# Two stores of a weight pipeline moved: sums stored a step after their last split, down weights handled two steps later

## The chip, the core and the metric

The kernel runs on one core of a Trainium2 chip. A core has a matrix engine (TensorE, PE in the profile), a vector engine (DVE), a scalar engine (ACT), GpSimd (POOL) and SyncE (SP), which here issues nearly all DMA transfers. Every engine works through its own list of instructions in order and waits at semaphores for the others; the transfers themselves run on 16 DMA engines beside them. The metric is the time of one execution on the device, in microseconds (us); lower is better.

## What is computed

Two layers of the same kind on an activation x of 2048 rows by 640 columns. Each layer is a Fourier mixing block followed by a gated feed-forward block, both with a residual:

```python
def _A_ref(x, dft_seq_re, dft_seq_im, dft_hid_re, dft_hid_im):
    a = jnp.einsum("bsd,ed->bse", x, dft_hid_re)
    b = jnp.einsum("bsd,ed->bse", x, dft_hid_im)
    return jnp.einsum("ts,bse->bte", dft_seq_re, a) - jnp.einsum("ts,bse->bte", dft_seq_im, b)

def _B_ref(x, w_gate, w_up, w_down):
    g = jnp.einsum("bsd,df->bsf", x, w_gate)
    u = jnp.einsum("bsd,df->bsf", x, w_up)
    return jnp.einsum("bsf,fd->bsd", _sigmoid(g) * u, w_down)

for layer in range(2):
    x = x + _A_ref(_layernorm(x), dft_seq_re, dft_seq_im, dft_hid_re, dft_hid_im)
    x = x + _B_ref(_layernorm(x), w_gate, w_up, w_down)
```

The hidden size of the feed-forward block is F = 1728: 13 tiles of 128 columns (j = 0 to 12) and a tail of 64 (j = 13). The weights are the same in both layers.

## The kernel before

**Precision by parts.** All large products run in f16 with each f32 number split in a high part HI and a rest LO; a product is three matmuls, HI by HI, HI by LO and LO by HI. `split` (L231 to 238) makes the parts of a weight: HI by one ACT instruction (L236), LO by one DVE instruction (L238).

**Blocks.** The feed-forward block treats the 2048 rows in four blocks of 512. In the first block of a layer, block 0, `gate_up` (matmuls at L1049) multiplies the rows with the gate and up weights themselves, one hidden tile j to a step: 30 matmuls of 512 columns for j below 13 and 15 for the tail; the first two of a step use the gate weight's HI part and the third is the first that needs its LO part. ACT then takes the sigmoid (L1063), DVE the product with the up half (L1064), and `gated_parts` splits the result into f16 (L1073 on ACT, L1074 on DVE) as tile `ht` of the hidden activation. Then `down` (L1242) multiplies the 14 hidden tiles with the down weights in eight steps, two for each 128 rows, and adds to x (L1257). In blocks 1 to 3, `seven` (L1095) forms gate and up with fewer products, from combinations of the weights, the "sums".

**What block 0 of the first layer does on the side.** It prepares every weight for the whole kernel:
- `load_w` fetches the f32 gate and up tiles (L954), the tail (L952) and the down tiles (L956, L959); `split_w` splits them; `keep_w` (and `gate_up` itself for gate and up) stores the f16 parts to DRAM as `kept_w`, through `keep` (L254).
- `make_sums` forms four sums of 256 columns of each gate and up tile on POOL (L998 to L1001), `split_sums` splits them in two pieces of 256 and 768 columns (L236, L238 again), and `keep` stores them as `kept_s`. For j of 3 to 12 the sums and their f16 parts have two fixed buffers each, by j even or odd (`take_sums`); the f32 gate and up tile is given back when its sums are made.

The same engines finish the mixing block beside it: `combine` (L920), `join_hidden` (L927) and `add_hidden` (L940) on DVE add its last rows to x, with a copy of one row on POOL (L938) between L940's first and second part. The tail of the hidden tiles is gated in `gate_tail` (L1225 to L1229).

Later blocks and the second layer only fetch `kept_w` and `kept_s` again (`load_s`, L1020 to L1023, and `load_w_again`). Before block 1 its activations are normalized, split and turned by DMA transposes (L516).

**What sets the order.** There is no automatic scheduler. `at(u, f, ...)` puts a job at a due time u, counted in steps; a loop at the end goes through the steps and, ahead of each step's matmuls, emits the jobs due in it, sorted by u. A gate/up step of block 0 has number `block[0] + j`. In the first layer the steps of j = 0 to 2 are written out by hand in an opening, so j = 3 is step 0, and jobs due earlier fall into step 0 as well. On each engine instructions stand in the order of emission, and so do the transfers in SP's queue: one that waits for its data keeps all that are behind it.

**Slots.** Most buffers come from one pool, `Slots`: `take` gives the free place that has been free longest among a few candidates, `drop` gives it back. A buffer's first writer so waits for whoever read the place last, which may be a store. Which places are used depends on the order of the jobs.

Due times before, with j the tile: gate/up loads at `block[0] + j - 4` and splits at `block[0] + j - 2` (j from 5 on); sums made at u = `block[0] + j - 1.5`, split at u + 1.55 (ACT) and u + 1.9 (DVE), stored in the same job; down loads at `block[0] + 0.8 j - 0.5`, splits at `+ 0.8 j + 1.6`, stores at `+ j + 4`.

All tiles on the chip are views of one large buffer, so the profile calls nearly all of them `big`.

Of the kernel before, what the change touches and what calls it, by code (L numbers as in the profile page):

```python
# [178 lines left out]
@with_exitstack  # L179
def kernel(ctx: ExitStack, tc: tile.TileContext, x, ct, wh, wg, wu, wc, wd, out):  # L180
    nc = tc.nc
    pool = ctx.enter_context(tc.tile_pool(name="sb", bufs=1))
    psum = ctx.enter_context(tc.tile_pool(name="ps", bufs=1, space=bass.MemoryType.PSUM))
    dram = ctx.enter_context(tc.tile_pool(name="dr", bufs=1, space=bass.MemoryType.DRAM))

    big = pool.tile([P, (UNITS + 2 * CK) * UNIT], F32, name="big")
    acc = [psum.tile([P, 512], F32, name=f"acc{i}") for i in range(6)]
    flag = pool.tile([P, 1], I32, name="flag")
    with tc.manual_schedule():
        folded(ctx, tc, pool, dram, big, acc, flag, x, ct, wh, wg, wu, wc, wd, out)  # L190
    bad = nc.values_load(flag[0:1, 0:1], min_val=0, max_val=1,
                         skip_runtime_bounds_check_because="it is the result of a comparison")
    with tc.If(bad != 0):
        with tc.manual_schedule():
            general(tc, big, [acc[2 * i : 2 * i + 2] for i in range(4)], x, ct, wh, wg, wu, wc, wd, out)


def folded(ctx, tc, pool, dram, big, acc, flag, x, ct, wh, wg, wu, wc, wd, out):
# [34 lines left out]
    def split(dh, dl, src, s, do=ALL):  # L233

        if 0 in do:
            nc.scalar.activation(dh, src, AF.Copy, scale=s)  # L236
        if 1 in do:
            nc.vector.scalar_tensor_tensor(dl, src, s, dh, op0=OP.mult, op1=OP.subtract)  # L238
# [13 lines left out]
    def keep(v, *key):  # L252
        kept[key] = dram.tile(list(v.shape), F16, name="kept_" + "_".join(map(str, key)))
        nc.sync.dma_start(kept[key], v)  # L254
# [5 lines left out]
    def at(u, f, *a):  # L260
        jobs[max(0, int(u // 1))].append((u, f, a))

    held = {}
# [16 lines left out]
    def drop(*key):  # L280
        s = held.pop(key if len(key) > 1 else key[0])
        if s.span:
            slots.give(s)
# [703 lines left out]
    def take_sums(key, j):  # L987

        if 3 <= j < NF:
            return fixed(XU + XTU + 16 * (j % 2) + 8 * (key == "sp"), 8, key, j)  # L990
        return take(8, key, j)
# [13 lines left out]
    def split_sums(j, do):  # L1005
        v, w = held["sf", j].f32, take_sums("sp", j) if 0 in do else held["sp", j]
        h, l = w.parts
        for c, sign in ((slice(0, 256), -WS), (slice(256, 1024), WS)):
            split(h[:, c], l[:, c], v[:, c], sign, do)
        if 1 not in do:  # L1010
            return
        drop("sf", j)
        keep(w.f16, "s", j)
        if j < 3:
            held["S", j] = held.pop(("sp", j))
        else:
            drop("sp", j)

    def load_s(j):
        nc.sync.dma_start(take(5, "G", j).f16, kept["w", 0, j])  # L1020
# [446 lines left out]
    for layer in range(2):  # L1467
# [10 lines left out]
        block = []  # L1478
# [81 lines left out]
        for b in range(1, NB):  # L1560
            for i in range(2):
                u = block[b] - 8 + 1.2 * i
# [9 lines left out]
        for b in range(NB):  # L1572
            for j in range(NF + 1):
                for q in ((0, j), (1, j)) if j < NF else ((3, 0),):
                    u = block[b] + j
# [12 lines left out]
            at(block[0] + j + (1.6 if j > 2 else 1.3), gated_parts, j)  # L1588
        for j in range(NF + 1):
            if first:  # L1590
                at(block[0] + 0.8 * j - 0.5, load_w, 2, j)
                at(block[0] + 0.8 * j + 1.6, split_w, 2, j)
                at(block[0] + j + 4, keep_w, 2, j)
            else:
                at(block[0] + j, load_w_again, 2, j)
                at(block[1] + j - 0.3, test_w, 2, j)

        if first:
            for j in range(NF):
                if 3 <= j < NF:  # L1600
                    u = block[0] + j - 1.5
                else:
                    u = block[1] - 8 + 1.5 * j
                    at(u - 2, load_sums, j)
                at(u, make_sums, j)
                at(u + 1.55, split_sums, j, (0,))
                at(u + 1.9, split_sums, j, (1,))
            at(block[0] + 12, close_slots)


# [8 lines left out]
        for q, (load, test, key) in enumerate(tests):  # L1619
            u = u0 + pace * q  # L1620
# [186 lines left out]
```

## Time and profile before

| | |
|---|---|
| median of three runs | 1168.69 us (1167.34 to 1170.28) |
| the profiled execution | 1166.17 us, span of the instructions 1164.4 us |
| mean granted TensorE clock in it | 0.995 |
| PE busy | 1128.2 us, 97% of the span |
| DVE, ACT, POOL busy | 738.8, 508.0, 149.5 us |
| moved by DMA | 216.40 MB, mean 186 GB/s |

Block 0 of the first layer stands on the time line from about 110 us (j = 3) to 184 us (start of the down steps); block 1 begins at 228.7 us.

How to read what follows. An entry of the timeline is start, duration, engine, source line, operation, tiles and how many instructions were merged; in square brackets stands how long the engine was idle ahead of it and what released it. SPq is SyncE's queue: an entry there is the issue of a transfer, not the transfer. An entry of the waits is engine and line, what was waited for, total us, how many times, the longest. A row of the windows is the stretch, its length, busy time of PE, PEld (weight loads), DVE, ACT and POOL with the number of instructions in brackets, the granted clock of TensorE, the busy share of the DMA engines and GB/s. Line numbers are those of the kernel before; in the changed kernel lines from L1013 on shift by two, and by four near the end.

### The profile page before, as it was taken

To read this page: it belongs to the slowest core of one execution; us is meant where nothing else is said; L and a number is where in the kernel's file an instruction comes from. 1 tells how busy PE (TensorE), PEld (TensorE's weight loads), DVE (VectorE), ACT (ScalarE), POOL (GpSimd) and SP (SyncE) were. 2 spreads that over 40 slices of the span, in tenths; PEclk is the share of its full clock that TensorE was granted. 3 is DMA by queue.
4 is the path that set the end of the run, shared out by engine and by line. 5 is a ranking of instruction groups with operands and counts; after the bars stand their busy time and mean duration, and the time that the engine had idled before them with its cause. 6 is when DMAs were issued, how large, how long until landed. Compare 5 with 4: busy or idle time off the path is not lost.

```text
span 1164.4 us, 22633 instructions
## 1 busy us (share of the span) xinstructions
PE 1128.2 (97%) x8784; PEld 859.6 (74%) x8784; DVE 738.8 (63%) x1636; ACT 508.0 (44%) x1094; POOL 149.5 (13%) x269
## 2 busy tenths in 40 slices
PE   5699999999999999999999999999999999999997
PEld 2467346788878887888776844678887888788875
DVE  7996698668656776676427566746974557524530
ACT  6865474155524653365304422315552455225420
POOL 2312486110001010100000001000000001000000
PEclk9999999999999999999999999999999999999998
DMA  9417698849595977769305442787849683667301
GB/s 275 138 46 231 228 350 295 240 136 262 160 240 149 263 211 192 220 222 253 94 1 169 169 129 67 197 236 229 253 148 243 223 268 133 139 211 236 121 18 38
DMA packets 225621, 216.40 MB, mean 186 GB/s; under 512 B 68034, under 2 KB 181851, under 8 KB 225502
## 3 DMA queue, kind: packets, MB, share of 16 engines
q1 hardware_dynamic: 224862, 212.23, 61.5%
q0 software_dynamic: 640, 2.62, 0.6%
q8 instruction: 71, 1.16, 0.4%
q14 instruction: 48, 0.39, 0.1%
HBM read 171.03 MB, written 30.40 MB: 173 GB/s over the span
## 4 chain that ended last, share of the span: by engine, by line
PE 93%; DVE 3%; DMA 2%; POOL 1%; SPq 1%; ACT 0%; issue 0%; DVEq 0%; POOLq 0%
PE acc L1095 40%; PE acc L1242 31%; PE acc L1049 14%; PE acc L855 4%; PE acc L1178 2%; PE acc L773 2%; DVE big L238 1%; DMA big<-in_ct 1%; DMA big<-in_x 1%; DMA big<-in_wh 1%; PE acc L523 0%; DMA big<-in_wd 0%; POOL quad L372 0%; DVE big L627 0%; DVE big L664 0%
## 5 line engine op out<-in xcount | busy, mean ns | idle before, releaser
L1095 PE MATMUL acc<-big 128*128 128x256 f16 x4212 | 463.1, 273 | 0.1
L1095 PEld LDWEIGHTS <-big 128*128 128x128 f16 x4212 | 412.0, 98 | 48.6 <-DMA big<-kept_w 0.3
L1242 PE MATMUL acc<-big 128*128 128x320 f16 x2624 | 357.7, 299 | 0.0
L1242 PEld LDWEIGHTS <-big 128*128 128x128 f16 x2624 | 256.7, 98 | 99.7
L1099 ACT ACTIVATE big<-acc 128x256 f32<-128x256 f32 x312 | 116.6, 381 | 208.8 <-PE acc L1095 207.4
L1049 PE MATMUL acc<-big 128*128 128x512 f16 (+1 forms) x990 | 178.1, 342 | 4.6 <-DVE big L238 4.6
L1049 PEld LDWEIGHTS <-big 128*128 128x128 f16 x990 | 96.9, 98 | 84.9 <-DVE big L238 5.6
L1275 ACT ACTIVATE big<-big 128x768 f32<-128x768 f32 (+8 forms) x104 | 79.4, 764 | 124.9 <-DVE big L1300 91.2
L1163 DVE TENSOR_TENSOR big<-big 128x512 f16<-128x512 f32 x78 | 53.8, 690 | 109.2 <-ACT big L1162 109.2
L1257 DVE SCALAR_TENSOR_TENSOR big<-acc,big 128x320 f32<-128x320 f32 x64 | 28.4, 484 | 93.5 <-PE acc L1242 93.4
L238 DVE SCALAR_TENSOR_TENSOR big<-big 128x640 f16<-128x640 f32 (+6 forms) x81 | 64.9, 842 | 0.5 <-ACT big L236 0.4
L1141 ACT ACTIVATE big<-big 128x512 f32<-128x512 f32 x78 | 47.8, 627 | 37.2 <-DVE big L1132 36.9
L1297 DVE TENSOR_TENSOR big<-big 128x256 f32<-128x256 f32 x64 | 26.6, 416 | 49.8 <-DMA big<-in_ct 49.8
L1132 DVE TENSOR_TENSOR big<-big,acc 128x512 f32<-128x512 f32 x78 | 53.1, 681 | 4.2 <-PE acc L1095 4.0
L1151 DVE SCALAR_TENSOR_TENSOR big<-acc,big 128x256 f32<-128x256 f32 x78 | 32.6, 418 | 35.1 <-PE acc L1095 30.8
L236 ACT ACTIVATE big<-big 128x640 f16<-128x640 f32 (+7 forms) x81 | 49.6, 664 | 6.7 <-POOL big L998 4.3
L1162 ACT ACTIVATE big<-big 128x512 f16<-128x512 f32 x78 | 48.8, 625 | 6.5 <-DVE big L1153 5.6
L855 PE MATMUL acc<-big 128*128 128x321 f16 (+3 forms) x324 | 49.0, 300 | 1.1 <-DVE big L238 1.1
L1064 DVE SCALAR_TENSOR_TENSOR big<-acc,big 128x512 f32<-128x512 f32 x26 | 17.9, 687 | 40.4 <-PE acc L1049 28.5
L855 PEld LDWEIGHTS <-big 128*128 128x128 f16 (+3 forms) x324 | 28.2, 95 | 20.3 <-issue 7.7
L509 ACT ACTIVATE big<-big 128x384 f16<-128x384 f32 (+2 forms) x48 | 28.9, 647 | 31.0 <-DVE big L491 26.7
L1063 ACT ACTIVATE big<-acc 128x512 f32<-128x512 f32 x26 | 15.4, 592 | 57.6 <-DVE big L1074 27.2
(183 smaller groups left out, 1001.5 us busy)
## 6 DMA issues: line engine op xcount, KB each, us to landing
big<-kept_w SPq DMA_DIRECT2D x125, 320.0 KB
big<-kept_s SPq DMA_DIRECT2D x75, 512.0 KB
big<-in_ct SPq DMA_DIRECT2D x256, 128.0 KB
big<-kept_w SPq DMA_DIRECT2D x78, 192.0 KB
kept_w<-big SPq DMA_DIRECT2D x41, 320.0 KB
big<-in_ct SPq DMA_DIRECT2D x32, 256.0 KB
kept_s<-big SPq DMA_DIRECT2D x13, 512.0 KB
big<-in_wg SPq DMA_DIRECT2D x16, 320.0 KB
```

The lines of the kernel that those rows point to most:

```text
L236: nc.scalar.activation(dh, src, AF.Copy, scale=s)
L238: nc.vector.scalar_tensor_tensor(dl, src, s, dh, op0=OP.mult, op1=OP.subtract)
L855: nc.tensor.matmul(ps[:m, :EC], z[:, at : at + m], w[:, 384 * wp : 384 * wp + EC], start=(d == 0 and zp == HI and wp == HI), stop=(d == ND ...
L1049: nc.tensor.matmul(ps, w[wp][:, d * P : (d + 1) * P], xt[:, xp, :], start=(d == 0 and wp == HI and xp == HI), stop=(d == ND - 1 and wp == LO))
L1095: nc.tensor.matmul(ps, wt, xt, start=start and n == 0, stop=n == len(todo) - 1, skip_group_check=not start)
L1099: nc.scalar.activation(dst, ps, AF.Copy)
L1132: nc.vector.tensor_tensor(v, v, other, op=OP.add)
L1141: nc.scalar.activation(v, v, AF.Sigmoid, scale=SG)
L1162: nc.scalar.activation(s.parts[HI], v, AF.Copy)
L1163: nc.vector.tensor_tensor(s.parts[LO], v, s.parts[HI], op=OP.subtract)
L1242: nc.tensor.matmul(held["pd", e][0][:, :EH], held["ht", j].parts[hp][:, i * P : (i + 1) * P], held["w", 2, j].parts[wp][:, e * EH : (e + 1 ...
L1275: nc.scalar.activation(v, v, AF.Square, accum_out=new_sum()[:p])
```

## The change

Two edits, both in the first layer's block 0. The number of instructions and transfers stays the same.

1. The store of the sums of j = 3 to 12 is taken out of the job that makes their last split and becomes a job of its own, `keep_sums`, due one step later. The buffer of the split sums is released with it. For j below 3 nothing changes.
2. The down weights' loads, splits and stores get later due times: at j = 0 by 2.7, 2.6 and 1.5 steps, at j = 13 by 2.0, 1.9 and 1.5.

```diff
         drop("sf", j)
-        keep(w.f16, "s", j)
         if j < 3:
             held["S", j] = held.pop(("sp", j))
-        else:
-            drop("sp", j)
+            keep(w.f16, "s", j)
+
+    def keep_sums(j):
+        keep(held["sp", j].f16, "s", j)
+        drop("sp", j)
...
             if first:
-                at(block[0] + 0.8 * j - 0.5, load_w, 2, j)
-                at(block[0] + 0.8 * j + 1.6, split_w, 2, j)
-                at(block[0] + j + 4, keep_w, 2, j)
+                at(block[0] + 0.75 * j + 2.2, load_w, 2, j)
+                at(block[0] + 0.75 * j + 4.2, split_w, 2, j)
+                at(block[0] + j + 5.5, keep_w, 2, j)
...
                 at(u + 1.9, split_sums, j, (1,))
+                if j > 2:
+                    at(u + 2.9, keep_sums, j)
```

## The prediction

> **What bounds the kernel.** I read the page's engine shares and chain first, then PE's waits in the first layer's block 0, then back from each wait along DVE, ACT and SyncE's queue.
>
> ```profile
> PE 1128.2 (97%) x8784; PEld 859.6 (74%) x8784; DVE 738.8 (63%) x1636; ACT 508.0 (44%) x1094; POOL 149.5 (13%) x269
> PE 93%; DVE 3%; DMA 2%; POOL 1%; SPq 1%; ACT 0%; issue 0%; DVEq 0%; POOLq 0%
> PE twin L350 <- ACT big L356: 11.2, 5, 7.7
> PE acc L1049 <- DVE big L238: 4.6, 2, 2.8
> ```
>
> TensorE sets the end. Of its waits, the transposes at L350 lie in the opening, which the change leaves alone. Waits of L1049 on L238 (gate/up products waiting for a weight's LO split on DVE) are the only ones in block 0; after 184 us the list of PE's waits is empty. So the change can win no more than what is lost here, and a loss needs a new PE wait.
>
> ```profile
> 96.43 39.59 PE L1049 MATMUL acc<-big 128*128 128x256 f16 x242
> 137.87 6.65 PE L1049 MATMUL acc<-big 128*128 128x512 f16 x30 [1.84 <-DVE big L238]
> 147.31 37.04 PE L1049 MATMUL acc<-big 128*128 128x512 f16 x163 [2.80 <-DVE big L238]
> 184.19 44.72 PE L1242 MATMUL acc<-big 128*128 128x320 f16 x328
> 144.00:148.00 4.00, 1.20 (x7) 0.36 (x6) 4.00 (x8) 1.44 (x3) 0.00 (x0) 1.00 1.02 360
> 148.00:152.00 4.00, 4.00 (x12) 1.48 (x11) 4.00 (x7) 2.58 (x5) 3.59 (x2) 0.57 0.74 253
> 152.00:156.00 4.00, 4.00 (x20) 1.84 (x19) 2.60 (x5) 0.72 (x2) 3.85 (x2) 1.00 1.00 352
> ```
>
> The 163 matmuls behind the second gap are 28 of j=8, 30 each of j=9 to 12, and 15 of the tail; so the gaps stand at the first LO matmul of j=7 and of j=8. In the windows (PE, PEld, DVE, ACT, POOL busy, then clock, DMA share, GB/s) the gap has a second price: from 148 to 152 the granted clock is 0.57, with 12 matmuls where the next 4 us hold 20. That costs 4.00 x (1 - 0.57) = 1.7 us. A step of 30 matmuls takes (37.04 - 1.7) / 163 x 30 = 6.5 us.
>
> [...]
>
> **Why DVE is late.** Queue issues, then ACT, DVE and POOL:
>
> ```profile
> SPq L254 <- DVE big L238: 20.4, 4, 8.2
> SPq L956 <- DVE big L920: 9.4, 2, 8.9
> 100.92 11.57 SPq L956 DMA_DIRECT2D big<-in_wd  x5
> 119.58 0.33 SPq L254 DMA_DIRECT2D kept_s<-big  x1
> 120.43 1.31 SPq L254 DMA_DIRECT2D kept_w<-big  x2
> 121.79 0.53 SPq L954 DMA_DIRECT2D big<-in_wg  x1
> 132.84 0.33 SPq L254 DMA_DIRECT2D kept_s<-big  x1
> 113.80 0.62 ACT L1073 ACTIVATE big<-big 128x512 f16<-128x512 f32 x1
> 125.47 0.60 ACT L1063 ACTIVATE big<-acc 128x512 f32<-128x512 f32 x1 [11.06 <-DMA kept_w<-big]
> 126.10 0.69 DVE L1064 SCALAR_TENSOR_TENSOR big<-acc,big 128x512 f32<-128x512 f32 x1 [6.59 <-ACT big L1063]
> 118.23 1.29 DVE L238 SCALAR_TENSOR_TENSOR big<-big 128x256 f16<-128x256 f32 x2
> 136.40 0.68 DVE L1064 SCALAR_TENSOR_TENSOR big<-acc,big 128x512 f32<-128x512 f32 x1
> 137.00 2.75 DVE L238 SCALAR_TENSOR_TENSOR big<-big 128x640 f16<-128x640 f32 x4
> 143.69 0.89 DVE L940 TENSOR_TENSOR big<-big 128x321 f32<-128x321 f32 x2 [2.07 <-POOL big L938]
> 132.02 1.37 POOL L998 TENSOR_TENSOR big<-big 128x256 f32<-128x256 f32 x1 [2.08 <-DVE big L238]
> 135.87 1.19 POOL L1001 TENSOR_TENSOR big<-big 128x256 f32<-128x256 f32 x1
> ```
>
> Read it backwards. The splits PE wanted at 136.02 began at 137.00, behind the gate product of j=4 at 136.40. That chain had started with the sigmoid of j=3 at 125.47, though PE had done j=3 by 136.0 - 0.4 - 3 x 6.5 = 116.1: its output slot is the one that w(1,3) leaves, and the store of that weight was not out. This store stood in SP's queue behind the first store of sums, which held the queue for DVE's split at 118.23, and behind five down-weight loads, two of which waited 9.4 us for L920. SP waits in order, so one early store of sums keeps a store that was ready long before; it went out at 120.43 and landed some 5.0 us on.
>
> **The change, part by part.**
>
> *Store of sums j (j of 3 to 12) a step on.* Ten issues, none added. By the built order, kept_w(3) (two stores) and the load of j=8 now stand ahead of kept_s(3), behind only three down-weight loads, whose slots don't wait for L920. Five issues took 11.57 - 9.4 = 2.2 us, three take 1.3; so kept_w(3) goes out at about 102.3 and lands by 107.3, ahead of 116.1. The sigmoid of j=3 is then bound by PE: 125.47 - 116.1 = 9.4 us earlier; DVE, whose work is the same, by its idle of 6.59 at least. Both gaps vanish if the split of j=8 comes 1.84 + 2.80 = 4.64 us earlier against PE. I take the lead between 6.6 and 9.4, so both go.
>
> What is late next? L940 on DVE waits for the row copy L938, which stands behind the sums of j=7 on POOL. One set of sums takes 135.87 + 1.19 - 132.02 = 5.0 us. The sums of j=5 start with the split of sums 3 (about 117), the copy follows, then j=6 and j=7: 117 + 3 x 5.0 + 2 x 0.7 = 133.4, where the trace has 143.69. Behind it on DVE stand L940, L1074, one down split, L1064 and the first split of w(8), four of 0.7 to 0.8 and one 0.9: about 137.4. PE wants it at 136.02 + 6.5 + 0.4 = 142.9. The margin is 5 us.
>
> The edit also adds a wait: the buffer of sums j is free a step later, so ACT's split of sums j+2 may stand for the store of j, behind the load of j+5, which waits for POOL's sums j+2. Behind it on ACT lie the down split, L1073 and L1063. One round is 5.0 (POOL) + 1.0 (issues) + 5.0 (landing, as of kept_w) + about 2 (HI split, first LO) = 13 us, against two PE steps of 13.0: even, with the lead in hand. I cost it at nothing; the ends are 0 (the buffer is never free earlier, so no gain) and rival E. On SP itself a down store, a down load and kept_w(j+1) are queued behind the store of sums j: fewer waits than before, since its split is a step old.
>
> *Down weights: loads, splits and stores two steps on.* Fourteen each, none added; each weight's split still stands two steps behind its load, so a late load would hold ACT at L236 with the sigmoid behind it. The latest by the allocator's slots is the load of down tile 7, behind POOL's sums of j=8: the split of sums 6 follows w(8) at about 139, sums 8 end at 144, and its split stands in the step of j=9, which begins at 136.02 + 2 x 6.5 = 149. Three splits that stood in step 0 ahead of sums 3 move behind it, so sums 3 is split some 2.4 us earlier, and DVE has as much more to do in the steady steps. The cover:
>
> ```profile
> L238 DVE SCALAR_TENSOR_TENSOR big<-big 128x640 f16<-128x640 f32 (+6 forms) x81 | 64.9, 842 | 0.5 <-ACT big L236 0.4
> 110.00:194.00 84.00, 79.36 (x387) 37.94 (x386) 68.58 (x93) 49.69 (x91) 53.22 (x58) 0.98 0.77 280
> 100.00:138.00 38.00, 36.16 (x212) 20.52 (x211) 22.13 (x34) 15.95 (x28) 9.04 (x9) 1.00 0.53 189
> 138.00:176.00 38.00, 35.20 (x156) 15.41 (x155) 34.51 (x44) 27.49 (x53) 29.64 (x25) 0.96 0.96 346
> 191.72 1.20 DVE L1229 TENSOR_TENSOR big<-big 64x512 f16<-64x512 f32 x1 [0.69 <-ACT big L1227]
> 186.15 0.63 ACT L1073 ACTIVATE big<-big 128x512 f16<-128x512 f32 x1 [3.84 <-DMA kept_w<-big]
> 210.86 7.27 SPq L516 DMA_TRANSPOSE big<-big  x2
> 219.36 0.48 SPq L1020 DMA_DIRECT2D big<-kept_w  x1
> ```
>
> DVE is busy 68.6 us from 110 to 194. If PE ends the block 6.3 us earlier, the same work has 77.7: 9.1 us of idle are allowed, where I count some 5 for the copy. At the block's end PE begins j=13 of the first row tile at 184.19 + 78 x 0.136 = 194.8 (0.136 = 44.72 / 328) and DVE had the tail ready at 192.92: 1.9 us of slack. This tail must come earlier too. It can: ACT stood 3.84 us for the store of w(1,11), behind a store of sums that is now behind it. If that cover fails, three splits of 0.84, 2.5 us, are lost.
>
> The DMA engines idled half the time before 138 and were full after it (0.96). The five early loads become three, which uses the idle stretch worse (2 x 0.33 MB); the freed loads and stores use it better. At 346 GB/s a moved store is 0.33 / 346 = 0.95 us of transfer. Later stores of down weights fall among the loads for block 1, whose first is issued at 219.36, 9.3 us ahead of PE's need; one store now stands behind it that stood ahead. Taken as nothing; ends 0 and, for three stores, 2.9 us.
>
> ACT's down splits move with DVE's and have more room (49.7 us busy in the 84). POOL's queue is unchanged. Slots in later blocks have other earlier holders; the trace's nearest row for what such a slot or load can cost PE is this:
>
> ```profile
> L1095 PEld LDWEIGHTS <-big 128*128 128x128 f16 x4212 | 412.0, 98 | 48.6 <-DMA big<-kept_w 0.3
> ```
>
> 0.3 us on a load, none on PE's own row; I take 0, with 0.3 either way.
>
> **Sum.** -1.84 - 2.80 - 1.7 = -6.3 us. The profiled execution is 1166.17 (span 1164.4), 2.5 below the median 1168.69; -6.3 makes 1159.9 there and 1162.4 on the median.
>
> **Rivals.**
> A, forecast: 1162.4; own range 1160.2 to 1164.
> [...]
> C, the lead is eaten by the copy on POOL or at the seam: the 1.84 goes, a wait like 2.80 with its slow clock stays, at j=8 or at the down steps: 1166.9. For it: only 1.9 us of slack at the tail, DMA 0.96 full.
> D, SP stands as long at other items (loads waiting for POOL's sums), so that nothing reaches PE: 1168.7. Against it: kept_w(3) passes everything that held it.
> E, slower: the buffer of sums. If a store of sums lands after 9 us and not 5, a round is 17 against 13; five rounds lose 20 us, less the 11 between a weight split's turn and its use (two steps, less 1.6 for two splits): 9 us of waits, in two gaps with 1.7 of slow clock each, so 12.4 over A, 1174.8. It eats A's gain from a landing of 7.8 us (5 x 2.8 - 11 + 3.4 = 6.4). Against it: the one landing that the trace prices is 5.0.
>
> **How the numbers follow.** Chances: A 0.60, B 0.08, C 0.12, D 0.06, E 0.14. A change under 0.3% (3.5 us) can't be told from none. Faster: B and A less 0.01 for its upper end, 0.67; same: C, D and that, 0.19; slower 0.14. The range holds A, B and C with 1.5 us of spread: 1160.2 to 1168.4.
>
> **What would show it.** After: L1049's waits on L238 gone or under 1 us; clock 1.00 across block 0; the sigmoid of j=3 near 116 and its DMA wait gone; kept_w(3) issued near 102; PE reaching the down steps (184.19) near 178 and block 1 (228.74) near 222.5. Wrong, if PE waits at 135 to 180 on L238 again, at L1242 for a down split or the tail, or at L1095 for block 1's loads or transposes; if ACT's L236 stands for kept_s, it is E.

## The result and the profile after

The changed kernel takes 1164.83 us (median of 22 runs, 1160.76 to 1169.09), the kernel before on the same chips 1167.19 (22 runs, 1165.46 to 1170.28). The ratio is 0.9977 with a 95% interval of 0.9966 to 0.9987: a gain of 2.4 us, where 6.3 were forecast and 1162.4 us expected. The profiled execution took 1161.90 us, 4.3 less than the one of before.

TensorE's time line of the changed kernel, from block 0 of the first layer to the last down steps (start, duration, what, and in brackets the idle time ahead with its releaser):

```profile
96.28 78.01 PE L1051 MATMUL acc<-big 128*128 128x256 f16 x420
174.65 0.60 PE L1051 MATMUL acc<-big 128*128 128x512 f16 x2 [0.36 <-ACT big L236]
175.51 2.98 PE L1051 MATMUL acc<-big 128*128 128x512 f16 x13 [0.26 <-DVE big L238]
178.32 44.72 PE L1244 MATMUL acc<-big 128*128 128x320 f16 x328
222.88 17.30 PE L1097 MATMUL acc<-big 128*128 128x256 f16 x157
...
407.25 13.93 PE L1097 MATMUL acc<-big 128*128 128x256 f16 x126 [1.45 <-DVE small L416]
...
1106.81 44.72 PE L1244 MATMUL acc<-big 128*128 128x320 f16 x328
```

Both waits of before (1.84 at j = 7, 2.80 at j = 8) are gone: 420 matmuls, up to the end of j = 12, run without a gap. Two things are new: 0.62 us at the tail's weights (j = 13), for ACT's HI split first, and 1.45 us in block 2 (the row names DVE; the same place in other profiles names a load of weights). The window in which the granted clock was 0.57 now has 1.00 and 20 matmuls:

```profile
148.00:152.00 4.00, 4.00 (x20) 1.85 (x19) 4.00 (x5) 2.62 (x5) 3.92 (x4) 1.00 0.78 267
```

The start of that is as the prediction put it. SyncE's queue and ACT in the changed kernel:

```profile
102.15 1.39 SPq L956 DMA_DIRECT2D big<-in_wd  x3
104.00 1.10 SPq L254 DMA_DIRECT2D kept_w<-big  x2
117.21 0.33 SPq L254 DMA_DIRECT2D kept_s<-big  x1
116.05 0.60 ACT L1065 ACTIVATE big<-acc 128x512 f32<-128x512 f32 x1 [3.67 <-PE acc L1051]
```

The store of w(1,3) leaves at 104.00, ahead of the first store of sums, and the sigmoid of j = 3 starts at 116.05, released by PE and no longer by a store. The down steps begin at 178.32 (184.19 before).

So this execution gained 5.87 us in block 0 and lost 1.45 in block 2. All profiles here can be read by three places. The first is the start of the first down steps. The second is PE's waits from there to the last down steps: less these, that stretch has 927.0 to 927.4 us in every profile but one (after: 1106.81 - 178.32 - 1.45 = 927.04; before: 1111.48 - 184.19 = 927.29; in the one with 929.0, that of the last eight late below, the 126 matmuls behind a wait of 3.12 take 15.60 us and not 13.9). The third is the end, from the start of the last down steps to the end of the execution: 1161.90 - 1106.81 = 55.1 after, 1166.17 - 1111.48 = 54.7 before. The question is why the median gained so much less than this execution.

### The profile page after: what moved, and what is told of

Same layout as the page of the kernel before. It is cut to its first block, busy times and chain, and to the rows that moved or that the text cites. A ratio compares the mean times of both kernels' runs of the same rounds, so it can differ in the third digit from the quotient of the medians.

```text
span 1160.1 us, 22627 instructions
## 1 busy us (share of the span) xinstructions
PE 1127.3 (97%) x8784; PEld 859.6 (74%) x8784; DVE 737.6 (64%) x1636; ACT 508.2 (44%) x1094; POOL 147.6 (13%) x269
## 4 chain that ended last, share of the span: by engine, by line
PE 81%; DMA 3%; POOL 2%; DVE 1%; issue 1%; ACT 1%; SPq 0%; POOLq 0%; DVEq 0%; ACTq 0%
PE acc L1097 36%; PE acc L1244 31%; PE acc L1051 8%; PE acc L855 2%; PE acc L1180 2%; PE acc L773 1%; DMA big<-kept_w 1%; DMA big<-in_ct 1%; POOL big L999 1%; POOL big L1000 1%; DMA kept_s<-big 1%; DVE big L238 0%; POOL big L998 0%; POOL big L1001 0%; DMA big<-kept_s 0%
## 5 line engine op out<-in xcount | busy, mean ns | idle before, releaser
L1101 ACT ACTIVATE big<-acc 128x256 f32<-128x256 f32 x312 | 116.1, 381 | 200.1 <-PE acc L1097 198.5
L236 ACT ACTIVATE big<-big 128x640 f16<-128x640 f32 (+7 forms) x81 | 50.7, 665 | 17.0 <-DMA kept_s<-big 7.7
L773 PE MATMUL acc<-big 128*128 128x256 f16 (+5 forms) x288 | 36.9, 288 | 2.6 <-DVE big L664 2.6
```

Source lines behind the costliest of these rows:

```text
L773: nc.tensor.matmul(o, xv[:, 384 * xp + c0 : 384 * xp + c0 + n], moving(r, cps[cp]), start=(i % 2 == 0 and r == 0 and xp == HI and cp == HI ...
L1101: nc.scalar.activation(dst, ps, AF.Copy)
```

## The experiments

All ratios are against the kernel before on the same chip, with 95% intervals; its medians there were 1167.82, 1168.10 and 1167.40 us in the three groups.

### Each edit alone, and both kernels again

The first edit alone: the kernel before with `keep_sums` and its due time, the down weights at their old times.

```diff
-                at(block[0] + 0.75 * j + 2.2, load_w, 2, j)
-                at(block[0] + 0.75 * j + 4.2, split_w, 2, j)
-                at(block[0] + j + 5.5, keep_w, 2, j)
+                at(block[0] + 0.8 * j - 0.5, load_w, 2, j)
+                at(block[0] + 0.8 * j + 1.6, split_w, 2, j)
+                at(block[0] + j + 4, keep_w, 2, j)
```

> The store of sums a step later alone, down weights as before. Theory one (the store of sums was what held SyncE's queue): kept_w(3) goes out when the five down loads let it, near 113, the sigmoid of j=3 starts by 119 where it was 125.5, PE's waits in block 0 fall from 4.6 us to under 1.5 and the down steps begin by 180.5; time 3 to 5 us below before in the profile. Rival (the down loads' own wait is what counts): waits of 3 us or more stay, time within 1.5 us of before.

The second edit alone: the kernel before with the three later due times (the diff above read backwards, without `keep_sums`).

> The down weights two steps later alone, the store of sums in the same job as its split, as before. Theory one: the store of sums 3 still stands ahead of kept_w(3) and of the load of j=8 and holds them to about 117.5, the sigmoid of j=3 starts near 122, later stores of sums hold the queue as before; one wait of 1 to 3 us stays in block 0; time 0 to 3.5 us below before. Rival: the down weights carry the gain, both waits go, the down steps begin near 178.

The changed kernel again, unedited, on the same chip:

> The changed kernel once more, for a second profile. Theory one: PE reaches the down steps of block 0 near 178 again, and what is missing between the 5.9 us won there and the measured gain is lost after block 0, at waits of PE on a weight load in blocks 1 to 3, which vary from run to run (0 to 4 us). Rival: in other executions the two waits of block 0 come back and the down steps begin at 180 or later.

And the kernel before again:

> The kernel before once more, for a second profile and for what the runs of one kernel differ by. Theory one: waits of 4 to 5 us in block 0 again with a stretch of half clock behind them, down steps near 184, at most 0.5 us of waits afterwards; ratio 1.000 within 0.15%. Rival: the waits in block 0 differ by more than 1.5 us between executions.

| kernel | median us | ratio |
|---|---|---|
| first edit alone | 1159.39 | 0.9922 [0.9907, 0.9937] |
| second edit alone | 1172.87 | 1.0042 [1.0025, 1.0058] |
| both | 1162.63 | 0.9950 [0.9935, 0.9965] |
| before | 1167.12 | 0.9996 [0.9985, 1.0007] |

The edits pull in opposite directions. The first gains 8.4 us against its group's 1167.82; the second loses 5.1 alone and 3.2 on top of the first. The sign of the second edit is clear: no run of the first edit alone (up to 1160.53) reaches those of both (from 1162.10). The sizes are less so: the changed kernel's own two ratios, 0.9977 above and 0.9950 here, lie 3 us apart with intervals that don't meet. TensorE in the first edit alone, then SyncE and ACT:

```profile
96.26 81.49 PE L1051 MATMUL acc<-big 128*128 128x256 f16 x435
177.59 44.72 PE L1244 MATMUL acc<-big 128*128 128x320 f16 x328
...
407.78 13.92 PE L1097 MATMUL acc<-big 128*128 128x256 f16 x126 [2.71 <-DMA big<-kept_w]
...
1107.33 44.72 PE L1244 MATMUL acc<-big 128*128 128x320 f16 x328
```

```profile
101.37 13.58 SPq L956 DMA_DIRECT2D big<-in_wd  x6
115.00 0.90 SPq L254 DMA_DIRECT2D kept_w<-big  x2
119.68 0.60 ACT L1065 ACTIVATE big<-acc 128x512 f32<-128x512 f32 x1 [5.44 <-DMA kept_w<-big]
```

Block 0 has no wait at all, though here the store of w(1,3) still stands behind six down loads (13.58 us, most of it a wait for L920) and the sigmoid of j = 3 still waits 5.44 us for it. Passing the store of sums alone brings the sigmoid from 125.47 to 119.68, 5.8 us, and that is enough for the 4.64 that PE lacked. The down steps begin 184.19 - 177.59 = 6.6 us earlier. So theory one holds, with a gain above its 3 to 5 us: 1166.17 - 1160.53 = 5.6 in the profile, 8.4 in the median.

Another 1.5 to 1.7 us lie at the end: its profile of 1160.53 us has 1160.53 - 1107.33 = 53.2 us there, where the kernel before has 54.7 and 54.9. This goes by kernel and not by execution: 54.7 to 55.7 in eight profiles (the kernel before twice, the second edit alone, the changed kernel twice, and below the third buffer in it, the late loads and the half sums), 53.0 to 53.3 in six (the first edit alone, and below the five others built on it). It lies behind the last store, which is issued at 1152.08 of a span of 1160.1 in the changed kernel and at 1152.61 of 1158.7 in the first edit alone. The page also lists the packets of a queue of the kind "instruction" (q14). The longer end goes with 48 of them and the shorter with 46 or 47, in thirteen of the fourteen profiles (the kernel with the late stores has 48 and the short end). That it is the cause wasn't tried. If the end is no effect of the schedule, which isn't shown either, these 1.9 us are to be taken off when schedules are compared: the second edit then costs 3.2 - 1.9 = 1.3 us on top of the first here.

The second edit alone keeps the gap at j = 8 (2.80 before, 2.66 here) and adds waits at j = 12, at the tail and, last, where the down steps reach the tail of the hidden tiles:

```profile
145.01 25.64 PE L1049 MATMUL acc<-big 128*128 128x512 f16 x118 [2.66 <-DVE big L238]
171.94 0.60 PE L1049 MATMUL acc<-big 128*128 128x512 f16 x2 [1.29 <-ACT big L236]
180.70 0.60 PE L1049 MATMUL acc<-big 128*128 128x512 f16 x2 [1.68 <-ACT big L236]
198.70 34.12 PE L1242 MATMUL acc<-big 128*128 128x320 f16 x250 [1.94 <-DVE big L1229]
```

Neither expectation of it holds. One of the two gaps stays, as theory one has it, but the time is 5.1 us longer and not up to 3.5 shorter.

The kernel before, profiled again, has gaps of 1.95 us at j = 7 and 1.12 at j = 8, and two later waits of 1.73 and 1.01 us. In block 0 that is 1.6 us less than in its first profile, and it is more than 0.5 us afterwards, so here its rival comes out.

The profiled execution of the changed kernel in this group was its longest one there (1167.55 us, where the median is 1162.63), and shows what a long execution has more than the first profile:

```profile
170.70 0.60 PE L1051 MATMUL acc<-big 128*128 128x512 f16 x2 [2.79 <-ACT big L236]
171.80 8.34 PE L1051 MATMUL acc<-big 128*128 128x512 f16 x30 [0.49 <-DVE big L238]
183.13 44.72 PE L1244 MATMUL acc<-big 128*128 128x320 f16 x328
```

The two gaps of before stay away, but the down steps begin at 183.13, so what this execution lacks is lost in block 0 (the rival) and not only behind it: at j = 12 ACT's split is 2.79 us late, and the 30 matmuls behind it take 8.34 us instead of 6.5. The two executions part at the second of POOL's sums of j = 8. POOL, SyncE and ACT of this execution, and then of the first profile:

```profile
144.12 4.64 POOL L999 TENSOR_TENSOR big<-big 128x256 f32<-128x256 f32 x1
151.51 0.33 SPq L956 DMA_DIRECT2D big<-in_wd  x1
163.90 1.78 ACT L236 ACTIVATE big<-big 128x256 f16<-128x256 f32 x3 [4.24 <-DMA kept_s<-big]
```

```profile
144.01 2.10 POOL L999 TENSOR_TENSOR big<-big 128x256 f32<-128x256 f32 x1
148.28 0.33 SPq L956 DMA_DIRECT2D big<-in_wd  x1
159.09 1.77 ACT L236 ACTIVATE big<-big 128x256 f16<-128x256 f32 x3 [1.33 <-DMA kept_s<-big]
```

A down weight's load waits in SyncE's queue for these sums (6.9 us in the longer execution), the stores of sums wait behind it, and ACT's split of later sums waits for the store of earlier ones. From that wait of 4.24 us to the late split at j = 12 ACT has no idle time left. This is the wait of rival E, the buffer of sums, and in this execution it costs 2.79 + 0.49 us of gaps and 1.8 of slow matmuls. In the first profile the same wait is 1.33 us and costs nothing; what is lost there is 0.62 us at the tail, where ACT's sigmoid ahead of the split waits for POOL:

```profile
173.37 0.60 ACT L1065 ACTIVATE big<-acc 128x512 f32<-128x512 f32 x1 [2.43 <-POOL big L1000]
```

### A third buffer for the split sums

In the changed kernel and in the first edit alone, the split sums take turns over three places instead of two.

```diff
-            return fixed(XU + XTU + 16 * (j % 2) + 8 * (key == "sp"), 8, key, j)
+            if key == "sp":
+                return fixed((XU + 20, XU + XTU + 8, XU + XTU + 24)[j % 3], 8, key, j)
+            return fixed(XU + XTU + 16 * (j % 2), 8, key, j)
```

> The changed kernel with a third buffer for the split sums, so that ACT's split of sums j+2 waits for the store of sums j-1 and no longer for that of sums j. Theory S (the late sums buffer is what the changed kernel loses against the first edit alone): ACT's waits at L236 for kept_s (7.7 us in the changed kernel's profile) vanish, PE has no wait above 0.5 us in block 0, the down steps begin near 178, and the median is 1159 to 1160.5. Rival L (the down weights' later loads and splits fill ACT, DVE and SP's queue in the last steps themselves): the median stays at 1162 to 1165, and ACT or DVE is late at j of 10 to 12 for another reason than kept_s.

> The first edit alone with a third buffer for the split sums. The first edit alone has 10.6 us of ACT's waits at L236 for kept_s, and no wait of PE in block 0, so both theories expect these waits of ACT to go and the time to stay at that of the first edit alone: 1158.5 to 1160.5.

ACT's waits at L236 for `kept_s` vanished in both, yet the changed kernel with it took 1164.61 us (ratio 0.9978 [0.9964, 0.9993]; without it 0.9977 and 0.9950). TensorE and one of ACT's waits (total, times, longest):

```profile
176.59 0.60 PE L1053 MATMUL acc<-big 128*128 128x512 f16 x2 [1.69 <-ACT big L236]
177.45 4.64 PE L1053 MATMUL acc<-big 128*128 128x512 f16 x13 [0.25 <-DVE big L238]
181.92 44.72 PE L1246 MATMUL acc<-big 128*128 128x320 f16 x328
```

```profile
ACT big L1067 <- POOL big L1002: 2.4, 1, 2.4
```

Theory S falls as an account of the whole loss: the wait at the tail is there without any wait for a store of sums, and the 13 matmuls behind it take 4.64 us instead of 2.98. ACT is late because the sigmoid (L1067 in this kernel, where the line of POOL is L1002 and not L1000) ahead of the tail's split waits 2.4 us for POOL, as it did in the first profile. The first edit alone with the third buffer took 1162.38 (0.9955 [0.9940, 0.9969]), 3 more than without and above the range of both theories. Its profile, of its shortest run at 1158.25, has no wait in block 0 and a granted clock of 0.999; the other four runs had 0.995 to 0.996 and took 1162.15 to 1163.92 us; where they lost the time stays open. As the third buffer so costs something of its own, it can't price the waits for `kept_s` in the changed kernel.

### Which part of the second edit costs

On top of the first edit: the later stores alone; then the later loads and splits alone.

```diff
-                at(block[0] + j + 4, keep_w, 2, j)
+                at(block[0] + j + 5.5, keep_w, 2, j)
```

> The first edit, and of the second only the down weights' stores 1.5 steps later; their loads and splits at their old times. Theory S: the stores pass nothing that ACT waits for, except that more of them stand ahead of the late kept_s: 1159 to 1160.5, as the first edit alone. Rival L: the same, since loads and splits are what it blames. A result of 1162 or more would say that the stores cost by themselves (up to 2.9 us, three stores among the loads for block 1).

```diff
+                at(block[0] + 0.75 * j + 2.2, load_w, 2, j)
+                at(block[0] + 0.75 * j + 4.2, split_w, 2, j)
+                at(block[0] + max(j + 4, 0.75 * j + 4.5), keep_w, 2, j)
```

> The first edit, and of the second only the down weights' loads and splits; their stores at the old time. Both theories place the loss in the loads and splits: 1162 to 1165, as the changed kernel, with ACT waiting at L236 for kept_s or DVE late at j of 10 to 12. A result of 1159 to 1160.5 would say that the stores make the loss.

Stores late: 1160.43 (0.9934 [0.9919, 0.9949]), as expected and not to be told from the first edit alone. Loads and splits late: 1164.46 (0.9973 [0.9957, 0.9989]), in the range expected and 4.0 more; by the two profiles 2.1 of them lie at the end (55.35 against 53.29), which leaves 1.9 for the blocks. Then these were divided by tiles (the lines shown for tiles 0 to 5; the second kernel has `j > 5`):

```diff
+                moved = j < 6
+                at(block[0] + (0.75 * j + 2.2 if moved else 0.8 * j - 0.5), load_w, 2, j)
+                at(block[0] + (0.75 * j + 4.2 if moved else 0.8 * j + 1.6), split_w, 2, j)
+                at(block[0] + j + 5.5, keep_w, 2, j)
```

> The first edit and the later stores; of the down weights, tiles 0 to 5 are loaded and split late as in the change, tiles 6 to 13 at their old times. Theory I (what costs is that the early tiles leave the stretch from 110 to 130 us in which DVE, ACT and the DMA engines have time): 1162 to 1165, DVE busy some 7 of 10 us from 120 to 130 and a wait of PE in the last steps. Theory T (what costs is that the last tiles stand ahead of the last weight splits): 1160 to 1161, as with the later stores alone (1160.4).

> The complement: tiles 6 to 13 are loaded and split late, tiles 0 to 5 at their old times. Theory I: 1160 to 1161, no wait of PE in block 0. Theory T: 1162 to 1165, with PE waiting for the tail's split behind ACT's sigmoid that waits for POOL.

The last eight late: 1160.07 (0.9934 [0.9914, 0.9954]), nothing lost. The first six late: 1168.61 (1.0017 [1.0002, 1.0031]), 8.5 above its complement with the same short end. That is beyond theory I's 1162 to 1165 and more than the whole second edit loses; here tiles 3 to 5 also fall among tiles 6 to 8, which kept their times, so the order among the tiles seems to count too. Theory I has the place right: it is the early tiles. What they leave is seen in the windows; first the first edit alone, then the changed kernel (the last two columns are DMA share and GB/s):

```profile
110.00:130.00 20.00, 20.00 (x94) 9.09 (x93) 18.15 (x28) 9.79 (x18) 7.45 (x8) 1.00 0.61 208
130.00:160.00 30.00, 29.94 (x140) 13.44 (x138) 27.42 (x36) 19.43 (x35) 21.64 (x18) 1.00 0.89 330
```

```profile
110.00:130.00 20.00, 20.00 (x94) 9.11 (x93) 17.12 (x28) 9.92 (x18) 11.13 (x9) 1.00 0.33 111
130.00:160.00 30.00, 30.00 (x141) 13.58 (x139) 27.02 (x36) 18.80 (x33) 21.42 (x18) 1.00 0.92 333
```

From 110 to 130 the DMA engines move (208 - 111) GB/s x 20 us = 1.9 MB less, in the one stretch that has room. By SyncE's queue this is three down loads of 0.33 MB fewer, and three stores of weights, two of them those of w(1,3), which left before 110. With the first six late, DVE is busy 7.12 us from 120 to 130, as theory I expected (8.81 in the first edit alone). But its mechanism, too little room later, isn't seen: in the stretch behind, from 130 to 160, DVE, ACT and POOL are busy less (22.90, 14.93 and 14.54 us against the 27.42, 19.43 and 21.64 above), since they wait. For what, ACT's waits say, here with the first six late, and below them TensorE's longest wait there:

```profile
ACT big L1075 <- POOL big L1001: 7.4, 1, 7.4
ACT big L1075 <- POOL big L1000: 4.3, 1, 4.3
```

```profile
167.52 0.61 PE L1051 MATMUL acc<-big 128*128 128x512 f16 x2 [3.13 <-ACT big L236]
168.38 17.46 PE L1051 MATMUL acc<-big 128*128 128x512 f16 x73 [0.25 <-DVE big L238]
185.67 44.72 PE L1244 MATMUL acc<-big 128*128 128x320 f16 x328
```

L1000 and L1001 are the last readers of an f32 up and gate tile. The sigmoid and the gated tile take places from `Slots`, and with the early down tiles late they get places that POOL's sums have just read. The sign is consistent: a wait of ACT's sigmoid or gated tile for POOL at L1000 or L1001 (2.4 us and more) stands in all six profiles of a kernel that handles the first six tiles late with full sums, and in none of the seven that handle them early. Whatever makes POOL late then makes ACT late, and the next weight split stands behind. This is read from the waits; it wasn't tried by itself.

### POOL's sums cut short

The changed kernel with the sums of j = 5 to 12 made on half their columns, so that the other half of them is left out.

```diff
+        n = 256 if j < 5 else 128
-        nc.gpsimd.tensor_tensor(s1, u[:, :256], u[:, 384:], op=OP.add)
+        nc.gpsimd.tensor_tensor(s1[:, :n], u[:, :n], u[:, 384 : 384 + n], op=OP.add)
...
```

> The changed kernel with POOL's sums of j = 5 to 12 made on 128 of their 256 columns; the other half of each buffer keeps the sums of two tiles before (so part of the computation is left out, and the later blocks get wrong sums). Theory P (what the changed kernel loses hangs on POOL: its sums come late beside DVE's splits, a down weight's load behind them holds SP's queue, and the sigmoid ahead of the last weight splits waits for the place that they read): POOL's sums from 140 to 178 take half the time, SP's and ACT's waits for them go, PE has no wait in block 0, the down steps begin at 177.6 and the median is 1158 to 1161. Rival L (ACT, DVE and the DMA engines have more to do in the late steps than fits): DVE's splits get somewhat shorter too, but the median stays at 1162 to 1165 with a wait on L236 or L238.

1161.82 us (0.9954 [0.9940, 0.9968]). ACT's sigmoid no longer waits for POOL, and block 0 has no gap. Some of the waits that theory P wanted gone are left, though: one of 2.4 us of ACT's L236 for POOL, and SyncE's for POOL's sums, which from 140 to 178 fall from 8.0 to 2.7 us. TensorE:

```profile
96.47 81.25 PE L1052 MATMUL acc<-big 128*128 128x256 f16 x435
177.55 44.72 PE L1245 MATMUL acc<-big 128*128 128x320 f16 x328
```

The down steps begin at 177.55, where theory P has 177.6. The median lies 0.8 above its range of 1158 to 1161, which took no account of the end: that is 55.7 us here, 2.5 more than in the first edit alone, and without those it would be 1159.3, the first edit's time (taken from the spans of the instructions, 1158.9 and 1158.7 us, the difference is 2.0 and the time 1159.8). Whether DVE's splits beside the shorter sums get shorter too, as rival L has it, isn't shown here; so this shows that POOL's sums are in the chain, not that they are all of it.

### A load for block 2 half a step earlier

```diff
-                        at(u - 2 - 0.5 * (j % 2) if j > 3 else
+                        at(u - 2 - 0.5 * (j % 2) - (0.5 if first and b == 2 and j == 11 else 0) if j > 3 else
```

> The first edit alone, with the load of the weights of j = 11 for block 2 of the first layer half a step earlier, ahead of the table loads that stood before it in SP's queue. The first edit alone has a wait of 2.71 us for it there, and all kernels here but one profile show 1.4 to 2.8. If that wait is the queue's order it goes, and the median falls from 1159.4 to 1157 to 1158; if the transfer itself is late (the DMA engines are full, or its place is not free), the wait stays and so does the time.

The wait in block 2 went, in the one profile there is, but the median of 1158.77 (0.9922 [0.9904, 0.9939]) has the ratio of the first edit alone and lies above the range expected. (The waits for it were not 1.4 to 2.8 us in all profiles but one, as the expectation says: the two with the third buffer have 0.56 and 0.60.)

```profile
379.76 42.18 PE L1097 MATMUL acc<-big 128*128 128x256 f16 x383
```

Its profiled run, the longest at 1160.73, has the down steps of block 0 at 180.51 because the stages ahead of block 0 ended some 2.6 us later in it (its 435 last matmuls began at 98.84, not 96.26); so it doesn't price the wait. This kernel and the first edit alone are the fastest here, ahead of both kernels compared.

## Why the prediction was right or wrong

**The number: inside the range, in part by luck.** 1164.83 lies in the range of 1160.2 to 1168.4, but above the 1160.2 to 1164 that forecast A gave itself; what holds it is the width added for rivals B and C. It is nearest to rival B's 1168.69 - 4.64 = 1164.1, both waits gone and the 1.7 us at a clock of 0.57 still there; but that clock went too, the window from 148 to 152 has 1.00. The forecast was also counted from 1168.69, the median of three runs; from the 1167.19 of 22 runs, -6.3 gives 1160.9, and the result is 3.9 above that. At 0.2% the gain lies under the 0.3% that the prediction itself took as its mark for telling a change from none. And the range's lower end isn't what 1.5 us of spread under 1162.4 gives, which is 1160.9.

**What bounds the kernel: right about block 0, too narrow about the rest.** The two waits were the loss in block 0 and went. That PE has no wait after 184 us was true of that execution only: the kernel before, profiled again, has 1.73 and 1.01 us in blocks 2 and 3, and of thirteen later profiles all wait 0.4 to 3.1 us in block 2 but the one whose load was moved. The sentence that the change can win no more than is lost in block 0 stood on one execution.

**The chain from SyncE over ACT to DVE: right, and its size.** 104.0 against 102.3 for the store, 116.05 against 116.1 for the sigmoid, 178.32 against 178 for the down steps, 222.88 against 222.5 for block 1, clock 1.00. The sum of -6.3 us was for block 0: the profile has -5.87, and the first edit alone -6.6. It is not the median's: of two profiled executions with both edits one reached it, and the other began its down steps at 183.13. The row copy on POOL came later than reckoned, with L940 behind it at 136.62 and not 133.4, which the margin of 5 us covered. And the gain was put down to passing the store of sums and two early down loads together; the store of sums alone does it.

**The added wait for the buffer of sums, costed at nothing: right for the first edit, not always for both.** ACT's L236 waits 10.6 us for `kept_s` in the first edit alone and TensorE has no wait in block 0. In the changed kernel it is 7.7 us without a cost in the first profile, and 9.7 in the longer execution, where 4.24 of them stand straight ahead of the loss at j = 12. The landing was taken as 5.0 us, that of a `kept_w`; from the issue of the store at 157.08 to the split at 163.90 it is 6.8, if that is the store that this split waits for. So E's sign showed, at some 5 us in that execution and not at 12.4.

**"Down weights two steps on", taken as nothing with ends 0 and 2.9: this step failed.** It costs 3.2 us on top of the first edit on the same chip, and by ratios of different groups and kernels (0.9973 to 0.9978 against 0.9922 and 0.9934) 4.6 to 6.5. Of each, 1.9 lie at the end, a term that no step of the prediction had; 1.3 to 4.6 are left for the waits that the profiles show in block 0. By its parts: the stores, to which the upper end was given, cost nothing, nor do the loads and splits of tiles 6 to 13; those of tiles 0 to 5 bring the waits. The prediction named the idle stretch ("the five early loads become three, which uses the idle stretch worse") and set an unmeasured gain against it. And it followed the places of the down loads only, up to POOL's sums of j = 8, not the places that ACT's sigmoid and gated tiles get when the order of takes changes. DVE's idle as cover was no answer either: what came late was ACT, behind POOL's sums or behind a store of sums that a down load waiting for them had held up.

**Rivals.** B falls: the clock of 0.57 went with the gap (1.00 from 148 to 152), so the changed kernel's profile does not show the 1.7 us that B keeps. C came near, a lead eaten behind POOL, but at j = 12 and the tail, not through the row copy. E's wait is there, as said above. D falls with the first lines of this profile, though the wait that it names, a load in SyncE's queue for POOL's sums, is part of the late loss.

**Open.** What makes the end 1.9 us longer in some kernels. Why executions of the changed kernel spread over 8 us (22 runs) where those of the first edit alone spread over 2 (5 runs). One start of it is seen, POOL's 2.10 or 4.64 us, but the slow form also stands in the first edit's 1158.25 run with the third buffer, where it does no harm. Two ways of being late are seen, ACT behind a store of sums (j = 12) and ACT's sigmoid behind POOL (the tail); which of them makes the median isn't known. That ACT's places make the difference is read from the waits; a kernel that moves those places alone wasn't tried.

## What to carry to other kernels

A job that is moved out of a busy queue leaves two marks to be costed: the engine time it takes elsewhere, and the places that everything allocated after it now gets; the second, as the waits here suggest, can put an engine behind one that it never waited for before (here ACT's sigmoid or gated tile behind POOL, for 2.4 us and more). Work that stands in an idle stretch is worth keeping there, even where it seems to block a store: cost each edit of a change alone, since here one gave 8 us and the other took back 3 to 6. A list of waits from one execution is a sample, here a low one, and the ends of two executions are to be compared too before a difference is put down to the schedule.

## What was not expected of the hardware

**The same sum on POOL took 2.10 or 4.64 us, the same splits on DVE 0.70 to 1.35.** DVE in the longer execution, and then in the first profile, at POOL's second sum of j = 8:

```profile
144.09 3.49 DVE L238 SCALAR_TENSOR_TENSOR big<-big 128x640 f16<-128x640 f32 x5
147.50 0.69 DVE L1076 TENSOR_TENSOR big<-big 128x512 f16<-128x512 f32 x1
148.10 1.35 DVE L238 SCALAR_TENSOR_TENSOR big<-big 128x640 f16<-128x640 f32 x1
```

```profile
143.98 1.55 DVE L238 SCALAR_TENSOR_TENSOR big<-big 128x640 f16<-128x640 f32 x2
145.82 3.24 DVE L238 SCALAR_TENSOR_TENSOR big<-big 128x640 f16<-128x640 f32 x3 [0.29 <-ACT big L236]
```

In the longer execution DVE has five splits back to back at 0.70 us each, and the L1076 behind them, beside a sum of 4.64 us; the sum ends at 144.12 + 4.64 = 148.76, and the split at 148.10 takes 1.35 us, about twice as long. In the first profile DVE has a break of 0.29 us ahead of 145.82, the sum ends at 144.01 + 2.10 = 146.11, and the three splits from 145.82 on take 1.08 on average. DVE had that break because ACT's split of the sums, which it waited for, began at 144.01 behind 2.10 us of waiting for a store; in the longer execution the store held ACT only 1.56 us, to 143.58. In this pair the store that came in sooner goes with the longer execution. What makes the sum longer in the one and three splits in the other isn't shown: no run moves one of the two rows alone.

**Matmuls ran slower behind some short gaps and not behind others.** Thirty matmuls of 512 columns took 8.34 us instead of 6.5 behind gaps of 2.79 and 0.49 us above, and 13 took 4.64 instead of 2.98 behind 1.69 and 0.25 with the third buffer. Behind one gap of 1.95 the same is seen in the kernel before, profiled again (granted clock 0.94 from 130 to 160):

```profile
138.43 8.34 PE L1049 MATMUL acc<-big 128*128 128x512 f16 x30 [1.95 <-DVE big L238]
```

Behind the gap of 1.84 in the first profile of before, 30 matmuls took 6.65 us (clock 1.00 from 136 to 144), and in block 2 gaps of 1.45 and 2.71 us left the 126 matmuls behind them at 13.9. In these profiles the length of the gap alone doesn't decide.
